# Delta-rule attention with a GELU layer: key norms read from the diagonal of the Gram blocks instead of from squares of K

## The chip, the cores and the metric

The kernel runs on one core of a Trainium2 chip. The metric is the device time of one execution in microseconds (us). The core has a matrix engine (PE, with its weight loads listed as PEld), a vector engine (DVE), a scalar engine (ACT), a general engine (POOL) and an engine that mostly issues transfers (SP). Each engine works through its own queue in order, and semaphores make one wait for another.

## The reference

```python
def _attn_ref(q, k, v, beta):                      # B=4, H=8, S=768, D=48
    k_n = k / (np.linalg.norm(k, axis=-1, keepdims=True) + 1e-06)
    state = np.zeros((B, H, D, D))
    for t in range(S):
        y[:, :, t] = einsum('bhd,bhde->bhe', q[:, :, t], state)
        v_old = einsum('bhde,bhd->bhe', state, k_n[:, :, t])
        state = state + beta_t * outer(k_n[:, :, t], v[:, :, t] - v_old)
# x = y as (3072, 384);  h = x @ w_in (384 x 2048);  out = gelu_exact(h) @ w_out (2048 x 384)
```

Every key is divided by its norm. The recurrence over 768 positions is solved in chunks, and its result goes through two matrix layers with an exact GELU between them. The two weights arrive as 64-bit numbers and are decoded to 32 bits on the chip.

## The kernel before

**Tiling.** The 768 positions are 12 chunks of 64. A chunk has two tiles, and a tile holds two batches: 2 x 64 positions on the 128 partitions, by eight heads. Two chunks in a row form a group, so a group has four tiles or 32 (tile, head) columns, and there are six groups, 0 to 5.

**One chunk.** `grams` multiplies the turned keys with themselves on PE (psG) and lets ACT copy the result: the off-diagonal 32 x 32 blocks into `G`, the diagonal ones into `diag` (L378, L382, L385). For a group, `eliminate_steps` inverts the triangular blocks on DVE. `flip` (L436) turns `diag` into `Nu`, so that one partition holds one whole 32 x 32 block as [row, column]. It is multiplied by `XM` (L437), which is the strict lower mask `low` times the row factors beta/norm^2, made on POOL (L431). Thirty row steps `eliminate(j)` follow, two DVE instructions each (L444, L446), then the diagonal is set to one, `weigh` multiplies by the column factors (L454), and `back` turns the result into `XM` and `Zf` (L460, L463). `top` copies part of `Zf` (L474), and `join` and `join_run` combine the 32-blocks to 64-blocks on PE (psJ).

**State.** `state_steps(w)` reads the state (psK, L578), forms `W` on DVE (L585), solves (psU), and computes outputs and the new state (psY; DVE adds `St`, L632, and `x`, L641). `turn` transposes `x` on PE (psX, L662) for the matrix layers.

**Norms before.** For groups 1 to 5 the norms come from squares of K: for chunks 2 and 3 ACT squares and sums head by head (L291, 32 times); for later chunks the keys are loaded a second time in natural layout (`Kn`), ACT squares a tile (L278), DVE sums it (L281), POOL takes the root as a power with exponent 0.5 (L306, 16 columns), and `factors` (L265 to L269) forms beta/norm^2. This is `prep` and `finish`, and it is done ahead of the Gram products. A small DVE transpose (L430) brings the factors into the layout of `Nu`. V is scaled by the norms on POOL or ACT (L332, L329). beta reaches its layout `beta_m` through 12 PE transposes in `signs`.

**Matrix layers.** For chunk c, `fc1` (psH, L684) and GELU on ACT (L686) make `G`. From chunk 2 on the second layer uses a scheme of seven products (psX, psZ, psY; L722) with additions on DVE: `mix` (L731 to L736) before the products, `read2` (L765 to L779) after. The last product into `psY` comes behind L768, which reads `psY` after the product before it.

**Order.** The start is written out by hand. The rest is a plan: each piece of work has a due time in units of chunks, and `emit` sorts by it. DVE keeps that order exactly; the other engines' orders come from a scheduler. I call step w the stretch with due times from w to w+1, in which the matrix layers of chunk w-1 run. In the trace step 3 is about 179 to 229 us, step 5 281 to 330, step 7 382 to 431, and step 9 483 to 532. In each of these four odd steps the elimination of a group (2, 3, 4, 5) runs on DVE between the other DVE work of the step; group 1 is eliminated at 120 to 149 us, behind the decoding of the weights, and group 0 at the start.

Of the kernel before, what the change touches and what calls it, by code (L numbers as in the profile page):

```python
# [8 lines left out]
F32 = mybir.dt.float32  # L9
U32 = mybir.dt.uint32  # L10
AX = mybir.AxisListType
ALU = mybir.AluOpType
# [4 lines left out]
def kernel(  # L17
# [28 lines left out]
    nc = tc.nc  # L46
    B, H, S, D = q.shape
    DM, DF = moe_w_in.shape
    C = 64
# [49 lines left out]
    for c in range(NC):  # L99
        for a in range(NA):  # L100
            u = tiles[c, a] = Unit()
            u.c, u.a, u.n = c, a, c * NA + a
            u.t = (c % 2) * NA + a
            if c < 4:
                u.Kp = u.Kn = Kp[u.n % NKS]
                u.Qp = Qp[u.n % NQS]
            else:
                u.Kn, u.Kp = Kp[2 + a], Kp[(4 if c % 2 == 0 else 0) + a]
                u.Kb, u.Qb = blocks_of[a], blocks_of[2 + a]
# [59 lines left out]
    nc.gpsimd.affine_select(out=low, in_=low, compare_op=ALU.is_ge, fill=0.0, base=-1,  # L169
# [4 lines left out]
    half = cpool.tile([128, NA * H], F32)  # L174
# [8 lines left out]
    beta_m = cpool.tile([128, NC, NA, H], F32)  # L183
# [71 lines left out]
    Ds, Gs, Nus, XMs, gms, ns = {}, {}, {}, {}, {}, {}  # L255
# [4 lines left out]
    def new_group(g):  # L260
        gms[g] = wk.tile([128, 2 * NA, H], F32, tag="gm", name="gm")

    def factors(gm, bt_, n):

        nc.vector.tensor_scalar_add(n, n, 1e-6)  # L265
        r = wk.tile([128, 2 * NA, H], F32, tag="r", name="r", bufs=1)[:, 0:n.shape[1]]
        nc.vector.reciprocal(r, n)
        nc.vector.tensor_tensor(gm, bt_, r, op=ALU.mult)
        nc.vector.tensor_tensor(gm, gm, r, op=ALU.mult)  # L269

    def squares(u, n, engine=None):
        kd = u.Kn[:, :, 0:D]
        if engine is nc.gpsimd:
            ksq = su.tile([128, H, D], F32, tag="w_e", name="ksq")
        else:
            ksq = wk.tile([128, H, D], F32, tag="ksq", name="ksq")
        if engine is None:
            nc.scalar.activation(ksq, kd, ACT.Square)  # L278
        else:
            engine.tensor_tensor(ksq, kd, kd, op=ALU.mult)  # L280
        nc.vector.tensor_reduce(n, ksq, axis=AX.X, op=ALU.add)  # L281

    def sum_of_squares(u, h):

        if "both" not in ns:
            n23 = wk.tile([128, 2 * NA, H], F32, tag="n0", name="n0", bufs=1)
            ns[2], ns[3] = n23[:, 0:NA], n23[:, NA:]
            ns["both"] = n23
        if h == 0:
            u.ksq = wk.tile([128, H, D], F32, tag="ksq", name="ksq")  # L290
        nc.scalar.activation(u.ksq[:, h], u.Kn[:, h, 0:D], ACT.Square,  # L291
                             accum_out=ns[u.c][:, u.a, h:h + 1])

    def prep(c):
        us = [tiles[c, a] for a in range(NA)]
        g = c // 2
        if c % 2 == 0:
            new_group(g)
        if c > 3:
            ns[c] = wk.tile([128, NA, H], F32, tag="n", name="n", bufs=4)  # L300
        n = ns[c]
        for u in us:
            if c > 3:
                squares(u, n[:, u.a])
        flat = n.rearrange("q a h -> q (a h)")
        nc.gpsimd.tensor_tensor(flat, flat, half, op=ALU.pow)  # L306

    def finish_both():
        factors(gms[1], beta_m[:, 2:4].rearrange("q c a h -> q (c a) h"), ns["both"])

    def finish(c):
        t = (c % 2) * NA
        factors(gms[c // 2][:, t:t + NA], beta_m[:, c], ns[c])
# [108 lines left out]
    def eliminate_steps(g):  # L422
        steps = []
        gts = []

        def scales():
            gt = wk.tile([128, HB], F32, tag="gt", name="gt", bufs=1)
            gts.append(gt)
            gl = XMs[g] = wk.tile([128, NU, HB], F32, tag="XM", name="XM", bufs=1)
            nc.vector.transpose(gt, gms[g].rearrange("q t h -> q (t h)"))  # L430
            nc.gpsimd.tensor_tensor(gl, low, gt.unsqueeze(2).to_broadcast([128, HB, HB]),  # L431
                                    op=ALU.mult)

        def flip():
            Nus[g] = wk.tile([128, HB, HB], F32, tag="Nu", name="Nu", bufs=1)
            nc.vector.transpose(Nus[g], Ds[g].rearrange("q u n -> q n u"))  # L436
            nc.vector.tensor_tensor(Nus[g], Nus[g], XMs[g], op=ALU.mult)  # L437
# [14 lines left out]
        def weigh():  # L452

            nc.vector.tensor_tensor(Nus[g], Nus[g],  # L454
                                    gts[0].unsqueeze(1).to_broadcast([128, HB, HB]), op=ALU.mult)
# [9 lines left out]
        steps = [(0.3, scales), (3.0, flip)]  # L465
# [5 lines left out]
    def top(g, p, us):  # L471

        part = Zf[g % 2][p * C:p * C + HB, us]
        nc.scalar.copy(part[:, :, 0:HB], part[:, :, HB:C])  # L474
# [365 lines left out]
    new_group(0)  # L840
# [12 lines left out]
    scales_, flip_, *rows, back0, back1 = [s_[1:] for s_ in eliminate_steps(0)]  # L853
    factors(gms[0], beta_m[:, 0:2].rearrange("q c a h -> q (c a) h"), n0)
    scales_[0]()
    flip_[0]()
    ng = wk.tile([128, NA, H], F32, tag="ng", name="ng", bufs=1)
# [3 lines left out]
    signs(2, NC)  # L861
# [32 lines left out]
    for p in range(2):  # L894
        top(0, p, EARLIER)
    for a in range(NA):
        join(0, (a,), 1)
    for p in range(2):
        top(0, p, LATER)
    for u in first[NA:]:  # L900
        scale_v(u)
    begin(0)
# [27 lines left out]
    def late():  # L930
# [3 lines left out]
        for a in range(NA):  # L934
# [3 lines left out]
            for c in range(5, NC, 2):  # L938
# [7 lines left out]
    sums = [(1.0, sum_of_squares, tiles[c, a], h) for c in (2, 3) for a in range(NA) for h in range(H)]  # L946
    plan += [at(1.08, 1.5, sums), at(1.51, 1.511, [(1.0, prep, c) for c in (2, 3)]), at(1.65, 1.655, [(1.0, finish_both)]), at(2.97, 2.971, [(1.0, finish, 4)]), at(2.725, 2.726, [(1.0, queries, third)]),
             at(1.12, 1.6, state_steps(1)),
             at(1.75, 2.45, eliminate_steps(1)),
             at(2.47, 2.6, top_steps(1, EARLIER) + top_steps(1, LATER)),  # L950
             at(2.64, 2.77, join_steps(1)), at(2.76, 2.985, state_steps(2)),
             at(2.72, 2.721, [(1.0, prep, 4)]), at(2.8, 2.9, [(1.0, grams, [tiles[4, a] for a in range(NA)])])]
# [5 lines left out]
    for c in range(4, NC):  # L958
# [5 lines left out]
        t = c - (2.1 if c % 2 == 0 else 2.6) if c > 5 else {4: 2.1, 5: 2.74}[c]  # L964
        plan += [at(t, t + 0.01, [(1.0, load_k, c, "Kn")])]
# [5 lines left out]
    for w in range(3, NC):  # L971
# [6 lines left out]
        if w % 2:  # L978
            plan += [at(w + 0.09, w + 0.092, gram + query), at(w + 0.25, w + 0.95, state_steps(w))]
            if two_ahead:  # L980
                rows = eliminate_steps(w // 2 + 1)
                plan += [at(w - 0.16, w - 0.15, [(1.0, prep, w + 2)]),
                         at(w, w + 0.01, [(1.0, finish, w + 2)]),
                         at(w + 0.13, w + 0.18, rows[:2]), at(w + 0.18, w + 0.36, rows[2:14]),
                         at(w + 0.4, w + 1.06, rows[14:-2]), at(w + 1.07, w + 1.16, rows[-2:]),
                         at(w + 1.17, w + 1.29, top_steps(w // 2 + 1, EARLIER)),
                         at(w + 1.305, w + 1.355, top_steps(w // 2 + 1, LATER))]
        else:
# [5 lines left out]
            if two_ahead:  # L994
                plan += [at(w + 0.35, w + 0.36, [(1.0, prep, w + 2)]),
                         at(w + 0.5, w + 0.51, [(1.0, finish, w + 2)])]
# [32 lines left out]
```

## Time and profile before

| | |
|---|---|
| median of three runs | 675.3 us (675.04 to 675.48) |
| the profiled execution, its own time | 674.69 us |
| its span, first to last instruction | 672.9 us |
| granted PE clock, mean | 0.982 |
| PE busy | 643.0 us (96%) |
| DVE busy | 419.9 us (62%) |
| ACT busy | 256.4 us (38%) |
| POOL busy | 75.8 us (11%) |

The page gives busy time by engine, the same in 40 slices of 16.8 us, the chain of work that ended last, and groups of instructions by line. A timeline row reads: start, duration, engine, line, operation, output <- input, count, and in brackets how long the engine stood idle ahead of it and what released it.

### The profile page before, as it was taken

Reading aid. Unit: us, or ns where it says so; the run is one execution under the profiler, and the core shown is the slowest. Engines: PE = TensorE matmul, PEld = TensorE weight load, DVE = VectorE, ACT = ScalarE, POOL = GpSimd, SP = SyncE. Lnnn points to the kernel's source line nnn. Section 1 sums busy time; section 2 is a strip of 40 time slices with the busy share of each in tenths; the row PEclk is TensorE's granted clock in tenths of the full one; section 3 lists DMA queues with packets and bytes.
Section 4 is the critical chain, followed back from the end, with each engine's and each line's share of the span. In section 5 each row is a group of like instructions: output and inputs, shape, how many; then the busy total and the mean of one; then the engine's idle time right before and its main releaser. Section 6 shows DMA issues by size and latency. Waiting matters only on the chain.

```text
span 672.9 us, 21675 instructions
## 1 busy us (share of the span) xinstructions
PE 643.0 (96%) x9542; PEld 562.7 (84%) x9542; DVE 419.9 (62%) x873; ACT 256.4 (38%) x654; POOL 75.8 (11%) x63
## 2 busy tenths in 40 slices
PE   6868999998999999999999999999999999999997
PEld 5656767766789989989989989989989979989997
DVE  6998989982699825479825479825479814324021
ACT  3477755624442173142173142173142153122220
POOL 4050301111211011111011111011111000000000
PEclk9976999998999999999999999999999999999999
DMA  8885655303531233511233411212301210100101
GB/s 119 186 251 172 120 165 136 48 1 56 91 50 31 50 47 54 84 27 31 51 47 56 82 26 31 48 21 35 63 3 31 50 18 3 24 2 2 23 1 24
DMA packets 158430, 39.75 MB, mean 59 GB/s; under 512 B 150016, under 2 KB 153216, under 8 KB 158336
## 3 DMA queue, kind: packets, MB, share of 16 engines
q1 hardware_dynamic: 152464, 33.40, 26.3%
q10 hardware_dynamic: 5872, 4.97, 3.2%
q8 instruction: 75, 1.23, 0.8%
q14 instruction: 19, 0.16, 0.1%
HBM read 33.62 MB, written 4.72 MB: 57 GB/s over the span
## 4 chain that ended last, share of the span: by engine, by line
PE 77%; DVE 14%; ACT 5%; issue 2%; DMA 1%; POOL 1%; SPq 0%; DVEq 0%; ACTq 0%; POOLq 0%
PE psH L684 32%; PE psX L722 12%; PE psY L722 12%; PE psZ L722 4%; PE psK L578 3%; DVE Nu L446 3%; DVE tmp L444 3%; PE psJ L525 3%; PE psG L367 3%; PE psU L600 2%; PE psO L697 2%; PE psY L618 2%; DVE w_e L235 1%; PE psY L627 1%; DVE w_out_sb L236 1%
## 5 line engine op out<-in xcount | busy, mean ns | idle before, releaser
L684 PE MATMUL psH<-xT,w_in_sb 128*128 128x256 f32 x1152 | 262.5, 384 | 3.8 <-ACT G L686 3.6
L684 PEld LDWEIGHTS psH<-xT,w_in_sb 128*128 128x128 f32 x1152 | 215.9, 190 | 35.9 <-ACT G L686 5.6
L686 ACT ACTIVATE G<-psH 128x256 f32<-128x256 f32 x192 | 73.2, 383 | 158.5 <-PE psH L684 157.6
L446 DVE TENSOR_TENSOR Nu<-Nu,tmp 128x30 f32<-128x30 f32 (+9 forms) x180 | 62.9, 349 | 6.2
L444 DVE TENSOR_TENSOR tmp<-Nu 128x30 f32<-128x30 f32 (+9 forms) x180 | 60.0, 333 | 5.2
L402 DVE TENSOR_TENSOR P<-psG,mask 128x1024 f32<-128x1024 f32 x10 | 12.2, 1224 | 80.4 <-PE psG L367 80.4
L722 PE MATMUL psX<-w_out_sb,G 128*128 128x192 f32 x320 | 56.2, 329 | 0.0
L722 PE MATMUL psY<-w_out_sb,G 128*128 128x192 f32 x304 | 54.1, 329 | 0.6
L722 PEld LDWEIGHTS psX<-w_out_sb,G 128*128 128x128 f32 x320 | 52.2, 190 | 0.7
L306 POOL TENSOR_TENSOR n<-n,half 128x16 f32<-128x16 f32 x10 | 29.4, 2944 | 197.9 <-DVE n L281 174.1
L663 ACT COPY xT<-psX 128x384 f32<-128x384 f32 x24 | 11.5, 479 | 105.2 <-PE psX L662 105.1
L722 PEld LDWEIGHTS psY<-w_out_sb,G 128*128 128x128 f32 x304 | 49.1, 190 | 2.1 <-DVE u L768 1.8
L697 PE MATMUL psO<-w_out_sb,G 128*128 128x384 f32 x128 | 45.7, 504 | 0.9 <-DVE w_out_sb L236 0.9
L697 PEld LDWEIGHTS psO<-w_out_sb,G 128*128 128x128 f32 x128 | 24.2, 196 | 16.0 <-DVE w_out_sb L236 1.5
L606 ACT COPY U<-psU 64x192 f32<-64x192 f32 x96 | 30.1, 314 | 19.5 <-PE psU L600 18.2
L332 POOL TENSOR_TENSOR V<-V,n 128x384 f32<-128x384 f32 x18 | 18.5, 1032 | 131.6 <-DMA V<-in_v_dram 92.7
L731 DVE TENSOR_TENSOR S<-G 128x512 f32<-128x512 f32 x20 | 14.4, 721 | 28.4 <-ACT G L686 28.4
L585 DVE TENSOR_TENSOR W<-psK,V 128x384 f32<-128x384 f32 x22 | 11.9, 554 | 31.3 <-ACT y L584 31.3
L641 DVE TENSOR_TENSOR x<-psY,y 64x192 f32<-64x192 f32 x80 | 28.3, 354 | 0.9
L722 PE MATMUL psY<-T,G 128*128 128x192 f32 x160 | 28.2, 329 | 0.0
L722 PE MATMUL psX<-T,G 128*128 128x192 f32 x160 | 28.1, 329 | 0.0
L722 PE MATMUL psZ<-T,S 128*128 128x192 f32 x160 | 27.6, 326 | 0.0
(138 smaller groups left out, 840.4 us busy)
## 6 DMA issues: line engine op xcount, KB each, us to landing
Kp<-in_k_dram SPq DMA_DIRECT2D x76, 96.0 KB, 3.3
w_out_sb<-in_moe_w_in_dram SPq DMA_DIRECT2D x24, 256.0 KB, 4.0
V<-in_v_dram SPq DMA_DIRECT2D x48, 96.0 KB, 3.1
out_dram<-o_sb ACTq DMA_DIRECT2D x46, 96.0 KB, 2.2
w_raw<-in_moe_w_out_dram SPq DMA_DIRECT2D x10, 384.0 KB, 4.6
Zf<-in_moe_w_out_dram SPq DMA_DIRECT2D x6, 384.0 KB, 4.2
Qp<-in_q_dram SPq DMA_DIRECT2D x64, 32.0 KB, 2.2
Qp<-in_q_dram SPq DMA_DIRECT2D x16, 96.0 KB, 3.8
```

Of the source, the lines that this page charges most:

```text
L306: nc.gpsimd.tensor_tensor(flat, flat, half, op=ALU.pow)
L367: nc.tensor.matmul(psG[HALF[p], r, i * NP + j, :], lhsT=u.Kt[rows, p, j, :], rhs=(u.Qt if x else u.Kt)[rows, p, j, :], start=True, stop=True)
L444: nc.vector.tensor_tensor(tmp, nu[:, j + 1:, j:j + 1].to_broadcast([128, n, j]), nu[:, j:j + 1, 0:j].to_broadcast([128, n, j]), op=ALU.mult)
L446: nc.vector.tensor_tensor(nu[:, j + 1:, 0:j], nu[:, j + 1:, 0:j], tmp, op=ALU.add)
L525: nc.tensor.matmul(psJ[to, i, :], lhsT=(xm if level else off)[rows, u, :], rhs=zf[rows, u, HB:C] if level else xm[rows, u, :], start=True, ...
L578: nc.tensor.matmul(u.psK[to, x, r, j, :], lhsT=(u.Qt if x else u.Kt)[rows, p, j, :], rhs=St[rows, u.a, p, j, :], start=True, stop=True)
L606: copy(pairs(u.U[HALF[p]], s), u.psU[HALF[p ^ s], p])
L641: nc.vector.tensor_tensor(dst, src, pairs(u.y[HALF[p ^ s]], s), op=ALU.add)
L684: nc.tensor.matmul(psH, lhsT=w_in_sb[:, f // 2, m, f % 2 * 128:(f % 2 + 1) * 128], rhs=xTs[c][:, m, :], start=(m == 0), stop=(m == NM - 1))
L686: nc.scalar.activation(G[:, f, :], psH, ACT.Gelu)
L697: nc.tensor.matmul(u.psO, lhsT=G[:, f, u.a * 128:(u.a + 1) * 128], rhs=w_out_sb[:, f, :], start=(f == 0), stop=(f == NF - 1))
L722: nc.tensor.matmul(ps_, lhsT=lhs[:, f, :], rhs=rhs[:, f, :], start=first and f == 0, stop=f == FH - 1, skip_group_check=not first)
```

## The change

In all groups but the first the norm of a key is read from the diagonal of its Gram block. `flip` now runs first, `norms` raises the 32 diagonal elements per partition of `Nu` to the power 0.5 on POOL, `scales` computes the factors in the turned layout, turns the norms back for V, and makes `XM`, and `scaled` multiplies the rows by the factors. The strict lower mask, now with its diagonal kept and combined with the column factors, is applied in `weigh`, behind the row steps. The second loads of K, the squares, their sums, `prep` and `finish` go away. beta of the later groups is loaded straight into the turned layout by 16 small transfers on SP's queue, issued after the keys of chunk 2 and ahead of the queries of chunk 2; ten PE transposes go. In the start, the `top` copies of group 0 move from ACT to DVE (first half) and POOL (second half). In the odd steps the due times become: flip and norms 0.11 to 0.12, scales 0.25, the mask-free scaling and four row steps 0.29 to 0.36, the other row steps and weigh 0.4 to 1.06; before, twelve row steps stood ahead of 0.36.

```diff
+    beta_t = cpool.tile([128, NG, HB], F32)
...
+    def load_beta():
+        for p in range(2):
+            for b in range(2):
+                for c in range(2):
+                    at_ = p * C + b * HB + c * NA * H
+                    for a in range(NA):
+                        src = beta[2 * a + p].rearrange("h (g t) -> h g t", t=2 * C)
+                        nc.sync.dma_start(out=beta_t[at_ + a * H:at_ + (a + 1) * H, 1:],
+                                          in_=src[:, 1:, c * C + b * HB:c * C + (b + 1) * HB])
...
         def flip():
             Nus[g] = wk.tile([128, HB, HB], F32, tag="Nu", name="Nu", bufs=1)
             nc.vector.transpose(Nus[g], Ds[g].rearrange("q u n -> q n u"))
-            nc.vector.tensor_tensor(Nus[g], Nus[g], XMs[g], op=ALU.mult)
+        def norms():
+            gts[g] = wk.tile([128, 2, HB], F32, tag="gt", name="gt", bufs=1)
+            flat = Nus[g].rearrange("q i c -> q (i c)")
+            nc.gpsimd.tensor_tensor(gts[g][:, 1], flat[:, 0:HB * HB:HB + 1], half, op=ALU.pow)
+        def scales():
...
+                factors(gts[g][:, 0], beta_t[:, g], gts[g][:, 1])
+                nc.vector.transpose(nat, gts[g][:, 1])
+            nc.gpsimd.tensor_tensor(gl, low, gts[g][:, 0].unsqueeze(1).to_broadcast([128, HB, HB]),
+                                    op=ALU.mult)
+        def scaled():
+            nc.vector.tensor_tensor(Nus[g], Nus[g],
+                                    gts[g][:, 0].unsqueeze(2).to_broadcast([128, HB, HB]), op=ALU.mult)
...
-            nc.vector.tensor_tensor(Nus[g], Nus[g],
-                                    gts[0].unsqueeze(1).to_broadcast([128, HB, HB]), op=ALU.mult)
+            nc.vector.tensor_tensor(Nus[g], Nus[g], XMs[g], op=ALU.mult)
...
-        steps = [(0.3, scales), (3.0, flip)]
+        steps = [(2.0, flip), (0.0, norms), (1.2, scales), (1.3, scaled)]
...
-    signs(2, NC)
+    load_beta()
...
     for p in range(2):
-        top(0, p, EARLIER)
+        top(0, p, EARLIER, nc.vector.tensor_copy)
...
+        top(0, p, LATER, nc.gpsimd.tensor_copy)
...
-    sums = [(1.0, sum_of_squares, tiles[c, a], h) for c in (2, 3) for a in range(NA) for h in range(H)]
-    plan += [at(1.08, 1.5, sums), at(1.51, 1.511, [(1.0, prep, c) for c in (2, 3)]), at(1.65, 1.655, [(1.0, finish_both)]),
+    second = eliminate_steps(1)
+    plan += [at(1.2, 1.21, second[:2]), at(1.5, 1.51, second[2:3]),
...
-        plan += [at(t, t + 0.01, [(1.0, load_k, c, "Kn")])]
...
-                plan += [at(w - 0.16, w - 0.15, [(1.0, prep, w + 2)]),
-                         at(w, w + 0.01, [(1.0, finish, w + 2)]),
-                         at(w + 0.13, w + 0.18, rows[:2]), at(w + 0.18, w + 0.36, rows[2:14]),
-                         at(w + 0.4, w + 1.06, rows[14:-2]), at(w + 1.07, w + 1.16, rows[-2:]),
+                plan += [at(w + 0.11, w + 0.12, rows[:2]), at(w + 0.25, w + 0.26, rows[2:3]),
+                         at(w + 0.29, w + 0.36, rows[3:8]),
+                         at(w + 0.4, w + 1.06, rows[8:-2]), at(w + 1.07, w + 1.16, rows[-2:]),
```

## The prediction

> **What bounds the kernel now.** I read the page's slices first, then busy time by stretch, then the timelines of DVE and PE inside one odd step, and last the queues of POOL and SP.
>
> The slices, PE and DVE:
>
> ```profile
> PE   6868999998999999999999999999999999999997
> DVE  6998989982699825479825479825479814324021
> ```
>
> The reader is to see that PE has spare time in the first slices only, and that DVE is nearly full in the 9s and 8s that come back every six slices. Those are the odd steps. Busy time by stretch (stretch, length, then PE, PEld, DVE, ACT, POOL, clock, DMA share, GB/s):
>
> ```profile
> 150.00:160.00 10.00, 6.72 (x180) 4.79 (x181) 0.59 (x1) 5.98 (x11) 2.34 (x1) 0.83 0.23 42
> 287.00:328.00 41.00, 40.88 (x570) 37.57 (x563) 35.33 (x84) 12.35 (x31) 3.89 (x3) 1.00 0.16 30
> 328.00:388.00 60.00, 60.00 (x1026) 54.14 (x1028) 27.96 (x58) 23.30 (x53) 7.99 (x4) 1.00 0.40 63
> ```
>
> From 160 us on PE is the bound and loses almost nothing (40.88 of 41, 60 of 60). So work taken from ACT, DVE or DMA there gains nothing, while whatever makes PE wait costs in full. PE waits 3.28 us at 150 us, behind the decoding and the elimination of group 1 on DVE. DVE in step 5:
>
> ```profile
> 289.43 1.99 DVE L436 STREAM_TRANSPOSE Nu<-diag 128x1024 f32<-128x1024 f32 x1
> 291.53 1.23 DVE L437 TENSOR_TENSOR Nu<-Nu,XM 128x1024 f32<-128x1024 f32 x1
> 292.79 0.21 DVE L444 TENSOR_TENSOR tmp<-Nu 128x30 f32<-128x30 f32 x1
> ...
> 302.44 0.69 DVE L731 TENSOR_TENSOR S<-G 128x512 f32<-128x512 f32 x1 [0.39 <-ACT G L686]
> ...
> 316.27 0.69 DVE L736 TENSOR_TENSOR G<-G 128x512 f32<-128x512 f32 x1 [0.61 <-PE psX L722]
> ...
> 326.61 0.36 DVE L768 TENSOR_TENSOR u<-psY,p 128x192 f32<-128x192 f32 x1 [1.44 <-PE psY L722]
> ```
>
> PE's next product starts at 327.03, right behind L768:
>
> ```profile
> 327.03 2.87 PE L722 MATMUL psY<-w_out_sb,G 128*128 128x192 f32 x16
> ```
>
> and the list of waits has it:
>
> ```profile
> PEld psY L722 <- DVE u L768: 1.8, 5, 0.4
> ```
>
> Between flip and L768 DVE stands idle for 0.39 + 0.61 + 1.44 = 2.44 us. That is all the delay an odd step can take before PE pays.
>
> **The odd steps.** In the changed order on DVE, `factors` stands directly behind `flip` and waits for POOL's power; nothing is between them, and the scaling, four row steps, W (L585) and the first additions for PE (L731) queue behind it. Flip cannot move up: it waits for the diag copy on ACT (L385, 288.16 + 1.24 = 289.40). Before, the root was taken a step ahead. The power's row, and POOL holding up DVE:
>
> ```profile
> L306 POOL TENSOR_TENSOR n<-n,half 128x16 f32<-128x16 f32 x10 | 29.4, 2944 | 197.9 <-DVE n L281 174.1 <-ACT ksq L291 23.9
> ```
>
> ```profile
> 305.58 1.04 POOL L332 TENSOR_TENSOR V<-V,n 128x384 f32<-128x384 f32 x1 [14.17 <-DVE Nu L446]
> ...
> 305.96 0.92 DVE L446 TENSOR_TENSOR Nu<-Nu,tmp 128x240 f32<-128x240 f32 x1
> ```
>
> - The power now has 32 columns. If its time were all fixed it would stay 2.9 us; if all per column it is 5.9. A POOL memset of 128x16 takes 0.11 us and a multiplication of 128x384 only 0.83, so little of the 2.9 is a fixed part, and I take 0.2 + 2 x 2.7 = 5.6 us.
> - The multiplication on POOL (XM, 1.92 us) is released together with the transpose of the norms and runs into the scaling. The row above shows a DVE instruction of 0.41 us stretched to 0.92 by the 0.66 us that POOL had left. With 1.7 us left I take 1.5 us; bounds 0 (before, XM ran beside flip and cost it nothing) and 1.9.
> - From flip's end to the first row step: signals 0.1 + 0.1, power 5.6, factors 0.97 (four instructions on 128x32 at 116.80 to 117.77), transpose 0.22, scaling 1.26, held up 1.5: 9.75 us, against 292.79 - 291.42 = 1.37 now. So 8.4 us later.
> - Ahead of L768 stand 25 row steps in place of 27. The two (130 and 108 wide) are 0.66 + 0.61 = 1.27 us.
> - PE pays 8.4 - 1.27 - 2.44 = **4.7 us** in step 5. Steps 7 and 9 have the same rows (DVE busy 35.35 and 35.31 of 41): 4.7 each.
> - In step 3 the gap before is 1.51 us, flip starts 0.15 earlier because `finish` is gone, and DVE idles only 0.94 us ahead of L768 (225.61): 9.75 - 1.51 - 0.15 - 1.27 - 0.94 = **5.9 us**.
> - In step 9 two instead of three copies of `top` (0.62 each) stand ahead of the GELU that PE waits for at 541.2 (1.54 us idle): -0.6.
>
> Sum 5.9 + 3 x 4.7 - 0.6 = **+19.4 us**. With the power at 2.9 it is 2.7 less in each step: +8.6. With that and no hold-up it is 1.7 + 3 x 0.5 - 0.6 = +2.6; with 5.9 and 1.9, +22.2.
>
> The Trainium skill (GPSIMD Engine Reference, section 3.1) puts two-input elementwise work at about 2.6 cycles per element. Read for the power, sixteen more columns would be an estimated 0.03 us, the power 2.9 us, and the whole 683 us by that rule against 694 by the row. But 16 columns in 2.9 us is far from that rate already, so I follow the row.
>
> **What goes away.** 16 squares on ACT (8.1 us), their sums on DVE (16 x 0.54), eight `finish` of 0.9 us, 32 key loads of 96 KB. From 160 us on these lie in stretches where PE is full and DVE and ACT are not (27.96 and 23.30 of 60), so I cost their loss at nothing; the loads land in 3.3 us and no engine's wait names them. The V scaling (L332) follows XM on POOL, which now ends near 300 us, before V at 305.58.
>
> **The start.** Until 153 us the chain is DVE's.
>
> - ACT loses 32 small squares that follow each other at 0.225 us (7.3 us). DVE waits for ACT's part of the decoding 0.50, 0.91 and 1.57 us; the last (87.82) vanishes, since `flip` of group 1 now sits in the decoding and fills it, and so does the 0.26 us wait for XM at 120.10: -1.8. All of DVE's idle from 45 to 121 us but a 1.15 us transfer wait would be some -4; that is the bound.
> - XM of group 1 now meets decoding: +1.5 (0 to 1.9).
> - Two squares between `top` and the join copies (151.14, 0.94 us): -0.9. Ten PE transposes at 18.8 us: nothing, PE idles there.
> - 16 beta transfers on SP. Rows of SP (start, time for all, count):
>
> ```profile
> 23.51 5.04 SPq L96 DMA_DIRECT2D Qp<-in_q_dram  x4
> 28.65 2.64 SPq L96 DMA_DIRECT2D Qp<-in_k_dram  x4
> 72.67 8.65 SPq L134 DMA_DIRECT2D Qp<-in_k_dram  x16
> 96.40 0.81 SPq L210 DMA_DIRECT2D w_raw<-in_moe_w_out_dram  x2
> ```
>
> An issue costs 0.40 to 0.54 us, so the queries of chunk 2, the keys of chunk 3, the weights and V behind them move back by 6.4 to 8.6 us. The keys land about 3.3 us after their issue, and PE turns them at 38.12 to 40.09 us: 0 to 3 us late, 1.6 in the middle. Behind them the Gram copies on ACT, and then XM's join copies (44.24), shift by as much; two `top` copies off ACT give 0.85 back ahead of the solve. +0.8 (-0.9 to +2.2). The later weights are decoded from 56 us on, still after they land.
> - Two `top` copies on DVE (on ACT 0.62 each): 1.2 to 2 us, covered by the 0.50 and 0.91 us waits; uncovered, up to +2.
>
> Sum -1.8 + 1.5 - 0.9 + 0.8 = -0.4, say -0.5, from -4.9 to +4.
>
> **Total.** +18.9 us on the profiled execution (674.69 us, 1.8 of it outside its span). The median lies 0.6 above it: 675.3 + 18.9 = **694**.
>
> **Rivals.**
> 1. *The power does not grow with the columns.* For it: ten powers at 2.90 us, almost to the ns, as a fixed part would give. Against: nothing else on POOL has a fixed part over 0.2 us. 675.3 + 8.6 - 0.5 = 683.
> 2. *Faster: the start gains more than the odd steps lose.* ACT's relief in the first 150 us removes DVE's waits, -4.9. It decides only where the odd steps cost less than that, so with a power below about 3.5 us and no hold-up by XM: 675.3 + 2.6 - 4.9 = 673. For it: 13.4 us of ACT work leaves a stretch in which PE and DVE wait for ACT. Against: the 2.44 us of slack.
> 3. *SP's queue decides the start.* Beta's issues wait for earlier landings too and push the keys of chunk 3 by 4 us and more: start +4 in place of -0.5: 698.5.
> 4. *The norms path is hidden after all*, if DVE had other work behind `flip`. The order on DVE has none, so I give it no chance of its own.
>
> **How the numbers follow.** Forecast 0.58, rival 1 0.17, rival 2 0.13 (0.09 of it faster, 0.04 within), rival 3 0.12. A measurement of this kernel tells about 0.2% (1.4 us) from no change. Faster 0.09, same 0.04, slower 0.87. The range goes from between rivals 2 and 1, 678, to just above rival 3, 700, and leaves out rival 2 and the tails. The forecast's own range is 690 to 699.
>
> **What would show it.** Right: the power row at 5 to 6 us on 128x32; DVE idle that long behind each `flip`, released by POOL; PE waiting for the addition to `u` in steps 3, 5, 7 and 9, with its busy share falling from 40.88 of 41 to about 41 of 46; the even steps unchanged. Wrong: a power near 3 us, or PE full in the odd steps. For the start: PE's wait at 150 us near 3 us as before, and a later first join if SP decides. The forecast fails most simply if the power has a large fixed part.

## The result: 3.5% slower, and the profile after

The changed kernel takes 698.57 us in the median (698.33 to 700.30, four runs), the kernel before beside it 675.39 us (675.04 to 675.55). The ratio is 1.0349, with a 95% interval from 1.0331 to 1.0367. The forecast was 694, with a range from 678 to 700.

The profiled execution of the changed kernel has a span of 696.6 us, 23.7 more than before. Where they lie is read by lining the two traces up at the state products (psK), which open the state part of every step. Difference of their starts, changed minus before:

| between | adds (us) |
|---|---|
| start of the trace and step 2 (psK at 163.18 before) | -1.73 |
| step 3 | +7.13 |
| step 5 | +5.76 |
| step 7 | +6.70 |
| step 9 | +5.81 |
| steps 4, 6, 8, 10 and the end, together | +0.05 |

So all of the loss is in the four odd steps, as forecast, and it is 25.4 us where the forecast had 19.4. Slices of PE and DVE of the changed kernel:

```profile
PE   6768999999997999999899999799999799999998
DVE  7999999943779815369924369825349934414121
```

PE now dips to 7 or 8 in one slice at each place where DVE has its 9s and 8s; before, it stood at 9 there. Busy time by stretch of the changed kernel, an even step and an odd one (columns as in the prediction):

```profile
236.00:288.00 52.00, 52.00 (x922) 47.04 (x921) 22.98 (x38) 20.26 (x46) 0.00 (x0) 1.00 0.35 53
288.00:343.00 55.00, 51.38 (x662) 46.47 (x662) 41.17 (x97) 13.75 (x35) 11.98 (x6) 0.97 0.14 27
```

The even step is full, the odd step has lost 3.6 us of PE and some of its clock (0.97). The power's row among the groups:

```profile
L409 POOL TENSOR_TENSOR gt<-Nu,half 128x32 f32<-128x32 f32 x5 | 27.4, 5475 | 358.3 <-DVE Nu L403 358.3
```

and the rows that are new in the list of waits (engine, tile and line, releaser, then the sum, the count and the longest):

```profile
DVE gt L274 <- POOL gt L409: 22.5, 4, 5.6
...
PE psY L711 <- DVE u L754: 7.2, 4, 1.8
PE psX L651 <- DVE x L630: 6.9, 4, 1.8
```

The power takes 5.5 us where 16 columns took 2.94, DVE stands still for it 5.6 us in each odd step, and PE waits twice for DVE at each odd step's end, for `x` (L641 before) and for the first of two additions to `u` (L765 before). Timeline of DVE behind `flip` in step 5 (L403 is flip, L274 begins the factors, L426 is the scaling, L434 and L436 are the row steps, L574 is W):

```profile
294.86 1.97 DVE L403 STREAM_TRANSPOSE Nu<-diag 128x1024 f32<-128x1024 f32 x1 [0.22 <-ACT diag L362]
302.45 0.18 DVE L274 TENSOR_SCALAR gt<-gt 128x32 f32<-128x32 f32 x1 [5.62 <-POOL gt L409]
...
303.52 1.21 DVE L426 TENSOR_TENSOR Nu<-Nu,gt 128x1024 f32<-128x1024 f32 x1
304.76 2.23 DVE L434 TENSOR_TENSOR tmp<-Nu 128x30 f32<-128x30 f32 x1
307.03 0.77 DVE L436 TENSOR_TENSOR Nu<-Nu,tmp 128x30 f32<-128x30 f32 x1
307.83 0.76 DVE L434 TENSOR_TENSOR tmp<-Nu 128x58 f32<-128x58 f32 x1
...
309.94 1.01 DVE L574 TENSOR_TENSOR W<-psK,V 128x384 f32<-128x384 f32 x2
```

and the timeline of POOL in the same stretch:

```profile
296.98 5.44 POOL L409 TENSOR_TENSOR gt<-Nu,half 128x32 f32<-128x32 f32 x1 [87.02 <-DVE Nu L403]
303.64 3.31 POOL L422 TENSOR_TENSOR XM<-low,gt 128x1024 f32<-128x1024 f32 x1 [1.22 <-DVE n L421]
306.91 1.61 POOL L309 TENSOR_TENSOR V<-V,n 128x384 f32<-128x384 f32 x2
```

The first three row instructions take 2.23, 0.77 and 0.76 us; alone they take 0.21, 0.21 and 0.22. They are over when POOL's three multiplications are. Timeline of PE at the end of step 5, where it now waits twice:

```profile
330.91 0.55 PE L651 MATMUL psX<-ident,x 128*128 128x128 f32 x3 [1.70 <-DVE x L630]
333.26 4.51 PE L711 MATMUL psY<-w_out_sb,G 128*128 128x192 f32 x16 [1.80 <-DVE u L754]
...
338.21 2.87 PE L711 MATMUL psY<-w_out_sb,G 128*128 128x192 f32 x16
```

Sixteen of the same products take 4.51 us behind the two waits, and the next sixteen take 2.87 us.

### The profile page after: what moved, and what is told of

The parts are those of the page before. It is cut to its first block, busy times and chain, and to the rows that moved or that the text cites. A ratio compares the mean times of both kernels' runs of the same rounds, so it can differ in the third digit from the quotient of the medians.

```text
span 696.6 us, 21515 instructions
## 1 busy us (share of the span) xinstructions
PE 654.0 (94%) x9532; PEld 570.1 (82%) x9532; DVE 423.4 (61%) x843; ACT 239.6 (34%) x568; POOL 79.9 (11%) x60
## 4 chain that ended last, share of the span: by engine, by line
PE 55%; DVE 33%; ACT 4%; issue 3%; POOL 3%; DMA 1%; SPq 0%; POOLq 0%; ACTq 0%; DVEq 0%
PE psH L673 21%; PE psY L711 11%; DVE tmp L434 9%; DVE Nu L436 7%; PE psX L711 7%; POOL gt L409 3%; PE psJ L514 3%; PE psG L344 2%; PE psZ L711 2%; PE psK L567 2%; PE psO L686 2%; DVE Nu L403 2%; DVE x L630 2%; DVE w_e L236 1%; DVE w_out_sb L237 1%
## 5 line engine op out<-in xcount | busy, mean ns | idle before, releaser
L434 DVE TENSOR_TENSOR tmp<-Nu 128x30 f32<-128x30 f32 (+9 forms) x180 | 73.2, 407 | 5.2
L711 PE MATMUL psY<-w_out_sb,G 128*128 128x192 f32 x304 | 62.1, 362 | 7.7 <-DVE u L754 7.2
L409 POOL TENSOR_TENSOR gt<-Nu,half 128x32 f32<-128x32 f32 x5 | 27.4, 5475 | 358.3 <-DVE Nu L403 358.3
L436 DVE TENSOR_TENSOR Nu<-Nu,tmp 128x30 f32<-128x30 f32 (+9 forms) x180 | 62.5, 347 | 6.2
L711 PEld LDWEIGHTS psY<-w_out_sb,G 128*128 128x128 f32 x304 | 56.3, 212 | 10.1 <-DVE u L754 8.2
L574 DVE TENSOR_TENSOR W<-psK,V 128x384 f32<-128x384 f32 x22 | 11.8, 554 | 31.3 <-ACT y L573 31.3
L711 PEld LDWEIGHTS psZ<-T,S 128*128 128x128 f32 x160 | 26.2, 190 | 1.8 <-DVE S L720 1.7
```

Of the source, the lines that this page charges most:

```text
L409: nc.gpsimd.tensor_tensor(gts[g][:, 1], flat[:, 0:HB * HB:HB + 1], half, op=ALU.pow)
L434: nc.vector.tensor_tensor(tmp, nu[:, j + 1:, j:j + 1].to_broadcast([128, n, j]), nu[:, j:j + 1, 0:j].to_broadcast([128, n, j]), op=ALU.mult)
L436: nc.vector.tensor_tensor(nu[:, j + 1:, 0:j], nu[:, j + 1:, 0:j], tmp, op=ALU.add)
L711: nc.tensor.matmul(ps_, lhsT=lhs[:, f, :], rhs=rhs[:, f, :], start=first and f == 0, stop=f == FH - 1, skip_group_check=not first)
```

## The experiments

All kernels below start from the changed kernel, and the short diffs are against it; "g < 2" and "g > 1" in them leave the start and group 1 as they are. Times are medians, ratios are against the kernel before on the same chip; the last column is what steps 3, 5, 7 and 9 add to the time before, read as in the table above. Five of the expectations below were missed by much: the root left out, the root for V only, both edits together and the early Gram products, which by their traces share one oversight (DVE idle ahead of W), and V on ACT.

| kernel | us | ratio (95%) | steps 3, 5, 7, 9 |
|---|---|---|---|
| changed kernel | 698.57 | 1.0349 (1.0331 to 1.0367) | 7.13, 5.76, 6.70, 5.81 |
| root left out | 684.00 | 1.0141 (1.0123 to 1.0160) | 2.63, 2.60, 2.68, 2.70 |
| root twice (two runs) | 718.77 | 1.0653 (1.0631 to 1.0674) | 12.32, 11.31, 11.18, 11.24 |
| column factors on DVE | 686.26 | 1.0175 (1.0153 to 1.0197) | 4.89, 3.39, 3.44, 2.37 |
| root for V only | 688.67 | 1.0208 (1.0193 to 1.0224) | 3.99, 3.85, 3.83, 3.89 |
| both of these | 687.79 | 1.0189 (1.0167 to 1.0212) | 3.83, 3.85, 3.84, 3.06 |
| Gram products early | 694.16 | 1.0290 (1.0254 to 1.0326) | 7.94, then see below |
| twelve rows ahead of W, alone | 704.70 | 1.0430 (1.0413 to 1.0447) | 8.67, 7.41, 7.20, 7.27 |
| twelve rows, root for V only | 682.71 | 1.0104 (1.0089 to 1.0119) | 3.15, 1.81, 1.81, 1.77 |
| twelve rows, both edits | 672.64 | 0.9961 (0.9948 to 0.9974) | 0.87, 0.01, 0.00, -1.38 |
| the same, V scaled on ACT | 681.82 | 1.0090 (1.0074 to 1.0105) | 2.22, 2.11, 2.14, 0.85 |

### The price of the root: left out, and taken twice

```diff
-            nc.gpsimd.tensor_tensor(gts[g][:, 1], flat[:, 0:HB * HB:HB + 1], half, op=ALU.pow)
+            nc.gpsimd.tensor_tensor(gts[g][:, 1], flat[:, 0:HB * HB:HB + 1], half, op=ALU.mult)
```

> The root of the squared norms is left out (POOL multiplies the 32 columns by 0.5 in place of raising them to the power 0.5), so the factors and V are scaled wrongly; everything else is the changed kernel. Theory (the wait behind flip makes the time, and the power is what is waited for): flip's end to the first row step falls by about 5.3 us in every odd step, the product that waits for u comes earlier by nearly as much, and the whole lands at 675 to 679 us in place of 698.6; PE's granted clock stays at 1.00 in the odd steps, because PE no longer stands still. Rival (POOL's multiplications that hold up DVE make the time, the power lies mostly in DVE's spare time): the whole stays above 688 us.

Measured 684.00 us. POOL's instruction now takes 0.26 us and DVE waits 0.44 us for it. The odd steps fall by 3 to 4.5 us each, less than the 5.3 taken away, and 2.6 us of each stay. PE's clock is back at 1.00 in step 5, though PE still waits there, 0.84 and 1.61 us for the two additions to `u`. The wait is thus the largest part and not the whole. What stays is POOL's hold-up of the row steps, as long as before (2.23, 0.77 and 0.76 us), and 1.9 us of idle time on DVE ahead of W and of the first addition for PE. The second kernel does the power two times:

```diff
-            nc.gpsimd.tensor_tensor(gts[g][:, 1], flat[:, 0:HB * HB:HB + 1], half, op=ALU.pow)
+            for _ in range(2):
+                nc.gpsimd.tensor_tensor(gts[g][:, 1], flat[:, 0:HB * HB:HB + 1], half, op=ALU.pow)
```

> The power is taken twice in a row on POOL in groups 1 to 5 (the second of the same input, so the result is the same). Theory: each odd step is longer by the full 5.4 us, since its spare time is used up already; 698.6 + 4 x 5.4 = 720.4 us. If a longer standstill of PE costs it more clock behind the standstill, some 1 to 2 us more in each step, up to 728. Rival (the power is partly hidden): below 715.

Measured 718.77 us: 20.2 us more for 4 x 5.5 us of added waiting. Nearly nothing of the wait is hidden. PE's granted clock does fall further (mean 0.940 in the profiled execution, 0.966 in that of the changed kernel), but no time comes on top for it. Another wait shows up, of the solve (psU) for W, in the timeline of PE in step 5:

```profile
321.12 1.96 PE L590 MATMUL psU<-W,Zf 64*64 64x48 f32 x64 [3.46 <-DVE W L575]
323.01 4.71 PE L712 MATMUL psX<-w_out_sb,G 128*128 128x192 f32 x16
```

Again the products behind the wait are slow: 4.71 us instead of 2.87.

### POOL's multiplication taken away

```diff
         def scales():
...
-            nc.gpsimd.tensor_tensor(gl, low, gts[g][:, 0].unsqueeze(1).to_broadcast([128, HB, HB]),
-                                    op=ALU.mult)
+            if g < 2:
+                nc.gpsimd.tensor_tensor(gl, low, gts[g][:, 0].unsqueeze(1).to_broadcast([128, HB, HB]),
+                                        op=ALU.mult)
...
         def weigh():
-            nc.vector.tensor_tensor(Nus[g], Nus[g], XMs[g], op=ALU.mult)
+            if g < 2:
+                nc.vector.tensor_tensor(Nus[g], Nus[g], XMs[g], op=ALU.mult)
+            else:
+                nc.vector.tensor_tensor(Nus[g], Nus[g], low, op=ALU.mult)
+                nc.vector.tensor_tensor(Nus[g], Nus[g],
+                                        gts[g][:, 0].unsqueeze(1).to_broadcast([128, HB, HB]), op=ALU.mult)
```

> In groups 2 to 5 the multiplication of the mask by the column factors on POOL is taken away; weigh does two multiplications on DVE instead of one, 1.2 us more, behind the last addition that PE waits for. Theory (POOL's multiplication holds up DVE's first row steps): the first three instructions of the row steps fall from 2.23, 0.77 and 0.76 us to about 0.2 each, unless the scaling of V, which then starts 3 us earlier, takes the place; each odd step is 2 to 3 us shorter, the whole 686 to 691. Rival (the hold-up is all of it): about 677. Rival (DVE's stretched instructions cost PE nothing): 698 to 699.

Measured 686.26 us, at the lower end of what was expected. DVE's first row instructions in step 5 take 0.70, 0.77 and 0.22 us; the scaling of V, which now stands right behind the power, holds the first two. Each odd step is 2.2 to 3.4 us shorter. In step 9, 1.2 of the 3.4 us have another source: PE waits 0.39 us in place of 1.59 for a GELU near the step's end, because ACT now does five GELUs and not four ahead of the `top` copies. The rest stays, so the hold-up is a cause in its own right.

### The wait taken away

The factor is beta / norm^2, and the squared norm is on the diagonal. No root is needed for it.

```diff
         def norms():
...
+            r = wk.tile([128, HB], F32, tag="r", name="r", bufs=1)
+            nc.vector.tensor_copy(gts[g][:, 1], flat[:, 0:HB * HB:HB + 1])
+            nc.vector.reciprocal(r, gts[g][:, 1])
+            nc.vector.scalar_tensor_tensor(gts[g][:, 0], beta_t[:, g], -1.0, r, ALU.mult, ALU.mult)
+            nc.gpsimd.tensor_tensor(gts[g][:, 1], gts[g][:, 1], half, op=ALU.pow)
...
         def eliminate(j):
             nu = Nus[g]
+            if g > 1 and j == 8:
+                nc.vector.tensor_scalar_add(gts[g][:, 1], gts[g][:, 1], 1e-6)
+                nc.vector.transpose(gts[g, "nat"], gts[g][:, 1])
```

The norms are turned back in front of the eighth row step (j == 8), not the ninth as the expectation has it.

> In groups 2 to 5 the factors come from the reciprocal of the squared norm itself (the 1e-6 added to the norm is dropped there), three short instructions on DVE right behind flip; POOL's power follows and serves only the scaling of V, and its result is turned in front of the ninth row step. Theory: the wait of 5.6 us behind flip is gone, flip's end to the first row step is 2 to 2.5 us, the hold-up by POOL stays; the whole 676 to 681 us. Rival (POOL's power, now beside DVE's row steps, holds these up for its 5.4 us): 690 or more.

And this edit and the one before it together:

> The two edits together in groups 2 to 5: the factors from the reciprocal of the squared norm (no wait for the power; the 1e-6 added to the norm is dropped there), and the mask and column factors by two multiplications on DVE in weigh (no multiplication on POOL). Theory: nothing is left that delays DVE by more than the 2.4 us that it has spare, PE does not wait in the odd steps, and only the 1.7 us that the start gained remain: 673 to 674.5 us, faster than the kernel before by 0.1 to 0.3%. If the scaling of V on POOL still holds DVE up by more than that: 675 to 680.

Measured 688.67 and 687.79 us: both far above the expectation, worse than leaving out the root, and next to nothing is gained by taking POOL's multiplication away as well. Timeline of DVE in step 5 of the second of the two (L447 and L449 are the row steps, L592 is W):

```profile
296.14 0.20 DVE L447 TENSOR_TENSOR tmp<-Nu 128x30 f32<-128x30 f32 x1
...
298.00 0.27 DVE L449 TENSOR_TENSOR Nu<-Nu,tmp 128x108 f32<-128x108 f32 x1
302.81 0.56 DVE L592 TENSOR_TENSOR W<-psK,V 128x384 f32<-128x384 f32 x1 [4.54 <-ACT y L591]
```

The row steps begin 2.13 us behind flip's end, unstretched, and then DVE stands still again, 4.54 us in front of W. In the changed order only four row steps stand ahead of W; before it was twelve. W cannot start before ACT has copied what PE makes at 301 us. The 5.6 us of waiting for POOL have turned into 4.5 us of waiting for ACT, and the eight row steps that could fill them stand behind it. POOL's multiplication fell into that idle time (299.94 to 302.30 in the kernel with the root for V only), and so it cost nothing there.

### Gram products earlier

```diff
-            plan += [at(w + 0.09, w + 0.092, gram + query), at(w + 0.25, w + 0.95, state_steps(w))]
+            ahead = gram if w > 3 else []
+            plan += [at(w - 0.09, w - 0.088, ahead)]
+            plan += [at(w + 0.09, w + 0.092, (gram if w == 3 else []) + query), at(w + 0.25, w + 0.95, state_steps(w))]
...
-                plan += [at(w + 0.11, w + 0.12, rows[:2]), at(w + 0.25, w + 0.26, rows[2:3]),
+                t = -0.06 if w > 3 else 0.11
+                plan += [at(w + t, w + t + 0.01, rows[:2]), at(w + 0.25, w + 0.26, rows[2:3]),
```

> The changed kernel with the Gram products of steps 5, 7 and 9 due 0.18 of a step earlier, ahead of the last product of the step before, and flip and the power with them; step 3 stays as it is. Theory (nothing is wrong with the power itself, only nothing stands on DVE while it runs): flip ends about 6 us earlier, in time in which DVE stands idle anyway, the power is over when DVE comes to the factors, and steps 5, 7 and 9 fall from +5.8, +6.7 and +5.8 us to 0 to 1.5 each, while step 3 stays at +7.1; the whole 680 to 685 us. Rival (a wait for the earlier Gram products takes its place on PE or DVE): above 690.

Measured 694.16 us: a miss. DVE does not wait for the power any more in steps 5, 7 and 9, and these cost 2.56, 2.55 and 2.80 us. But in front of each of them 3.86, 1.96 and 1.98 us are lost. (The profiled execution took 698.09 us and was the slowest of the four; in front of its step 5 PE waits 2.00 us, and the granted clock is 0.89 from 285 to 300 us.) Ahead of its step 7 the timeline of PE has

```profile
397.04 0.55 PE L651 MATMUL psX<-ident,x 128*128 128x128 f32 x3 [0.88 <-ACT xT L652]
```

and in that step the timeline of DVE has

```profile
417.00 0.56 DVE L574 TENSOR_TENSOR W<-psK,V 128x384 f32<-128x384 f32 x1 [3.46 <-ACT y L573]
```

ACT's Gram copies now stand between the copies (xT) that PE's last products of the step before wait for, and DVE idles in front of W as above, because there are four row steps to do.

### The order ahead of W

```diff
-                         at(w + 0.29, w + 0.36, rows[3:8]),
-                         at(w + 0.4, w + 1.06, rows[8:-2]), at(w + 1.07, w + 1.16, rows[-2:]),
+                         at(w + 0.29, w + 0.36, rows[3:16]),
+                         at(w + 0.4, w + 1.06, rows[16:-2]), at(w + 1.07, w + 1.16, rows[-2:]),
```

This diff stands in all four kernels of this part. First alone, with the wait and POOL's multiplication as they are:

> The changed kernel with its wait, and twelve row steps ahead of W in place of four, nothing else. Theory (the four go with the wait: behind 5.6 us of waiting there is no time for more ahead of W): W comes some 5 us later than now, PE waits in front of the solve as well, and two more row steps stand ahead of the last addition to u; each odd step is 1.2 to 3 us longer, the whole 703 to 711 us. Rival (the order alone is the cost): 690 or less.

Measured 704.70 us, as expected by the theory. PE waits for W in front of the solve, 17.9 us in all four steps together, 4.16 in step 5. So four row steps are the better number as long as the wait is there: the order and the wait belong together. Then without the wait, POOL's multiplication still there ("the run with that multiplication on DVE" is the one after this):

> Factors from the reciprocal of the squared norm in groups 2 to 5 (the 1e-6 dropped there), twelve row steps ahead of W, and the multiplication by the column factors still on POOL, behind the power. Theory: against the run with that multiplication on DVE, POOL's 3.3 us now meet the row steps ahead of W and hold them up by 2 to 3 us, more than is spare: each odd step costs 2 to 3 us, the whole 681 to 686. Rival (the hold-up falls into spare time): 673 to 676.

Measured 682.71 us. POOL and DVE meet in front of W in step 5. Timeline of POOL:

```profile
294.76 5.43 POOL L416 TENSOR_TENSOR gt<-gt,half 128x32 f32<-128x32 f32 x1 [83.17 <-DVE r L414]
300.15 2.43 POOL L431 TENSOR_TENSOR XM<-low,gt 128x1024 f32<-128x1024 f32 x1
```

and of DVE (L441 adds the 1e-6 for V's norms):

```profile
296.13 0.20 DVE L446 TENSOR_TENSOR tmp<-Nu 128x30 f32<-128x30 f32 x1
...
300.28 2.34 DVE L441 TENSOR_SCALAR gt<-gt 128x32 f32<-128x32 f32 x1
```

Beside the power DVE's row steps run at their usual 0.20 us. Beside the multiplication an instruction of 0.17 us takes 2.34, to the end of POOL's. Now without either:

> As the run without the wait and without POOL's multiplication (factors from the reciprocal of the squared norm in groups 2 to 5, the 1e-6 dropped there; mask and column factors on DVE in weigh), and now twelve row steps stand ahead of W, as in the kernel before, in place of four. In that run DVE stood idle 4.54 us ahead of W, because only four row steps stood there. Theory (wait, hold-up and the order ahead of W together make the odd steps' cost): the idle time ahead of W fills with eight row steps of about 0.6 to 0.8 us; DVE is then later than in the kernel before by 0.7 us at the first row step, 0.4 for turning the norms and about 1.2 for four scalings of V on POOL in place of two, 2.3 us against 2.4 us that are spare. Each odd step costs 0 to 0.7 us, the whole is 673 to 676 us. Rival (something else in the new order costs, such as the instructions behind W): 680 or more.

Measured 672.64 us (671.52 to 673.86, seven runs), just below the expected range and 0.39% faster than the kernel before (0.26 to 0.52%). Step 5 is as full as before in busy time (columns as above):

```profile
285.00:327.00 42.00, 41.89 (x625) 38.19 (x623) 35.88 (x85) 12.13 (x32) 8.96 (x5) 1.00 0.11 22
```

and in its timeline DVE waits for PE again, and not PE for DVE:

```profile
326.60 0.36 DVE L775 TENSOR_TENSOR u<-psY,p 128x192 f32<-128x192 f32 x1 [0.86 <-PE psY L729]
```

DVE has 0.86 us to spare ahead of the addition that PE waits for; before it had 1.44 there. This is the version that beats both. Its lead of 2.9 us over the kernel before is not explained in full, and what the traces show of it is not the norms. The span of its profiled execution is only 1.1 us shorter than before: the start gives 0.91 us, within its own spread (see below), and step 9 gives 1.38, while steps 3, 5 and 7 add 0.88 and the even steps 0.31. In step 9 it is PE's wait for the GELU that falls, from 1.54 to 0.36 us. In all four kernels with both multiplications of `weigh` on DVE, ACT does five GELUs ahead of the `top` copies there, and this wait is 0.32 to 0.39 us; in all the others ACT does four, and it is 1.54 to 1.62. So that gain goes with an order on ACT that came along with the edit and was not its aim. Taking POOL's multiplication away was worth 0.9 us with four row steps ahead of W (less than those two runs can tell apart) and 10.1 us with twelve, some 1.2 of these by that order. The last step was to take V off POOL too ("the first of these four" is the run of 672.64 us):

```diff
-  plan += [at(c - 0.4, c - 0.3, v_steps(c)) for c in range(4, NC)]
+  plan += [at(c - 0.4, c - 0.1, [(1.0, scale_head, tiles[c, a], h)
+                                 for a in range(NA) for h in range(H)]) for c in range(4, NC)]
```

> As the first of these four, and V of chunks 4 to 11 is scaled on ACT, head by head, in place of POOL. Theory: the last hold-up of DVE by POOL in the odd steps goes (about 2.2 us), DVE has spare time again, PE waits nowhere in the odd steps, and the whole is 672.5 to 674.5 us, 0.1 to 0.4% faster than the kernel before. If the 64 small scalings hold up ACT's GELUs between PE's products: 675 to 680.

Measured 681.82 us, a little worse than the second of the two cases named. ACT waits 2.91 us for V to land (306.41) with GELUs queued behind it, and the timeline of PE shows the wait for ACT:

```profile
307.52 1.56 PE L691 MATMUL psH<-xT,w_in_sb 128*128 128x256 f32 x6 [1.40 <-ACT G L693]
```

### The start

Beta's transfers moved behind the weights and V:

```diff
-    load_beta()
     for u in first:
         transposed(u, (1,))
...
     load_v(1)
+    load_beta()
```

> The changed kernel with the 16 beta transfers issued behind the weights and V of the start in place of ahead of the queries of chunk 2. Theory (SP's queue delays loads that PE can wait for, and the start is set by DVE): PE's waits for the queries and keys of chunk 2 and 3 at 34 to 39 us go, the first state product moves by less than 0.5 us and the whole by less than 1 us: 697.8 to 698.7. Rival (the beta transfers cost the start): 696 to 697.

The four `top` copies of group 0 back on ACT:

```diff
-        top(0, p, EARLIER, nc.vector.tensor_copy)
+        top(0, p, EARLIER)
...
-        top(0, p, LATER, nc.gpsimd.tensor_copy)
+        top(0, p, LATER)
```

> The changed kernel with the four copies of top of group 0 back on ACT. Theory: they are worth the 0.5 us by which the first solve came earlier, and the wait of DVE for ACT that covers it afterwards; the whole is longer by 0 to 1 us: 698.6 to 699.6. Rival (DVE pays for its two copies): shorter by up to 1.5 us.

Measured 699.29 us (698.58 to 700.18) and 697.97 us (696.60 to 700.41), ratios 1.0363 (1.0345 to 1.0380) and 1.0343 (1.0318 to 1.0368). The first lies 0.6 us above its expected range, the second in that of its rival, and neither can be told from the changed kernel's 1.0349. With the transfers late PE's waits for the loads go, as expected, and the Gram products start at 38.34 us in place of 40.02; but the first join behind them starts at 43.14 in both, when DVE has `XM` ready. The start itself is not the same from one profile to the next: in the profiles of the changed kernel and of the eight others whose edits leave the start alone (without the two of the root, which change group 1), the psK of step 2 comes 0.24 to 3.40 us earlier than before. So for either edit the intervals rule out an effect of more than some 3 us on the whole, and what is smaller stays open.

## Why the prediction was right, point by point

The total was right (698.57 in the range of 678 to 700, and just inside the forecast's own 690 to 699), and so were the mechanism and its place. That the total came as near as this is partly luck, since errors cancel: in step 5 the forecast had DVE 1.8 us too late at the first row step and nothing for 3.3 us of hold-up behind it, and the start gained 1.2 us more than it had. By the total alone rival 3 (698.5) would have been right; the profile decides against it, for the loss lies in the odd steps.

| step 5, us | forecast | measured |
|---|---|---|
| power of 32 columns | 5.6 | 5.44 |
| flip's end to the first row step | 9.75 (1.5 of it hold-up) | 7.93 (294.86 + 1.97 to 304.76) |
| later than before by | 8.4 | 6.6 |
| further hold-up of DVE by POOL, more than before | 0 | 3.3 |
| two row steps fewer | -1.27 | -1.13 |
| spare time of DVE | -2.44 | -2.44 (none is left) |
| DVE late at the last addition to u (L757, L768 before) | 4.7 | 5.8 (40.97 behind flip's end, 35.19 before) |

The terms of the right column (6.6, 3.3, -1.13 and -2.44) add up to 6.3; neighbouring rows overlap by up to 0.1 us at their ends, so a sum of rows is off by some tenths.

- **The power grows with the columns.** Right: 2.94 us for 16, 5.44 for 32, that is 0.16 us a column and 0.4 fixed. Rival 1 falls. Its ten powers "at 2.90 us, almost to the ns" were nine; one, at 77.71 us, took 3.32. The figure of the Trainium skill (GPSIMD Engine Reference, section 3.1: about 2.6 cycles per element) would have left the power near 2.9 by the prediction's estimate; the measurement decides against it for this operation.
- **POOL holds up DVE.** The mechanism was right, but the term was too small and in the wrong place: 1.5 us for the scaling, with 1.9 as the upper bound. The scaling (1.21 us) was not held at all. It had started 0.12 us ahead of POOL's multiplication, which took 3.31 us where it had taken 1.91, as if it waited for the scaling's end; then DVE's first row instruction waited for POOL. Two scalings of V right behind cost another 1.1. The forecast had V follow only at 305.58, where it cost nothing more than before. Taking the multiplication alone away gave 12 us (686.26).
- **PE pays what DVE is late.** Right for step 5, though PE does not wait where the forecast had it, at the last addition to `u`, but ahead of it: twice, 1.70 and 1.80 us, and the next 16 products then take 4.51 us. In step 5 DVE comes to the last addition no earlier than these end, so this hides. In step 7 the products take 5.49 us, DVE waits 1.03 us for them, and the step costs 6.70. The forecast had no term for it. The difference of about 0.9 us between steps 5 and 7 is not fixed to a place: in the two kernels of the start step 9 is dear (6.66 and 6.67), and step 3 has 7.95 and 7.94 in place of 7.13. It goes with PE's clock. Over 20 us at the end of a step the mean granted clock is 0.83 in every dear step (step 7 here, steps 3 and 9 in those two) and 0.91 in all the others of the three kernels. With a clock of one half in between, that is about 6.8 and 3.6 us of slow clock (twice the missing share of 20 us).
- **Step 3 costs more than step 5**: forecast by 1.2, measured by 1.4. **Step 9 costs 0.6 less**: not seen, and the reading behind it was wrong. Two copies of `top` in place of three do stand ahead of that GELU, but they start when DVE has `Zf` ready, and PE still waits 1.59 us (1.54 before). In the best version three copies stand there, and the wait is 0.36, because ACT does one GELU more ahead of them (see above).
- **Even steps unchanged, no cost for what is gone**: right, +0.05 us together.
- **The start**: PE is busy for 8.45 of the 10 us behind 150, where it was 6.72; its wait for the join there is 1.55 us in place of 3.28. Forecast -0.5, measured -1.73 in the profile. Group 1's elimination ends 0.77 us earlier on DVE (147.80 against 148.57), and the two squares in front of the join copies were worth 0.96. The two waits of DVE forecast to vanish (at 87.82 and 120.10) did; POOL's multiplication held a decoding instruction for 2.0 us (2.99 instead of 0.96), forecast 1.5. Beta's transfers took 7.08 us on SP (forecast 6.4 to 8.6) and made PE wait for the queries and keys, 1.09, 1.50 and 0.47 us, but the Gram products of the keys start at 40.02 in both traces. So rival 3 falls, and rival 2 with its short power as well. How much of the 1.2 us between forecast and measurement is the start's own spread is open.
- **A rival's price was wrong.** The forecast priced a kernel with a short power and no hold-up at +2.6 us in the odd steps (rival 2). The kernel with no wait and no multiplication on POOL has even less for DVE to wait for, and its odd steps cost 14.6. The forecast counted the row steps ahead of L768 (25 for 27) and not those ahead of W (4 for 12). As long as DVE waits for POOL this does not matter. Without that wait it is nearly all that is left, and only with twelve row steps back ahead of W does the time fall below the kernel before.

## What to carry to other kernels

On an engine that works in order, a wait is paid until something else sets the same end: before pricing its removal, look for the next instruction that has a fixed earliest time (here W, which needs PE's product through ACT) and count the work that stands ahead of that one, not only ahead of the end. Price single edits in the order in which they would stay: one and the same edit was worth 1 us, 10 us or 12 us, depending on what else was there. And a value that is needed squared does not have to wait for its root: the root can follow for the consumer that has time.

## What the runs showed of the hardware that was not expected

**PE's clock behind short waits.** In the changed kernel PE waits 1.70 and 1.80 us with 0.55 us of work between. Stretches of it behind these waits, in steps 5 and 7 (columns as above, the granted clock is third from the end, in front of the DMA share):

```profile
333.00:338.00 5.00, 4.74 (x19) 4.58 (x19) 4.56 (x14) 0.00 (x0) 0.00 (x0) 0.66 0.00 0
...
440.00:445.30 5.30, 5.28 (x16) 5.19 (x17) 4.13 (x12) 0.00 (x0) 0.00 (x0) 0.50 0.02 3
```

PE is busy and runs at 0.66 and 0.50. In the kernel without wait and multiplication, four row steps ahead of W, PE waits 1.80 and 1.62 us in steps 3, 5 and 7, with 2.87 us of products between, and the clock behind the waits in step 5 is 1.00. But in step 9 of the same execution the first of these waits is enough. Timeline of PE, and the stretch around it:

```profile
538.53 4.55 PE L729 MATMUL psY<-w_out_sb,G 128*128 128x192 f32 x16 [1.80 <-DVE u L772]
```

```profile
536.00:546.00 10.00, 8.00 (x38) 7.40 (x38) 9.21 (x29) 1.25 (x3) 0.00 (x0) 0.83 0.05 11
```

So the length of the waits alone does not decide it in these runs. Where PE waits 4.16 us for W (twelve rows alone), the products behind take 4.79 us. The Trainium skill (TensorE: Matmul & The Clock Gate, Part 1) says that the clock falls to one half after an idle window of about 3.4 us and that the window's place is not fixed to the program. The half agrees (0.50), and so do the 3.6 and 6.8 us of slow clock worked out above, about one and two such windows. That a wait of 1.80 us can be enough does not agree with a whole idle window, and here the measurement decides; whether the place of the window makes the difference between steps no run here shows. What these runs add is the price. The 16 products behind such waits take 1.6 to 2.6 us more. Where DVE is late anyway, little of it is seen in the time: in the kernel with the root for V only, step 3 has it (4.55 us for the 16 products) and costs 3.99, and steps 5 and 7 do not and cost 3.85 and 3.83. Where it lasts twice as long, it costs 0.8 to 1.1 us more (steps 3, 7 and 9 of the changed kernel against the same steps of the two kernels of the start).

**POOL's power does not hold up DVE, POOL's multiplication does.** Both work on tiles in SBUF. Beside the power DVE's row steps keep their 0.20 us; beside the multiplication a DVE instruction waits until POOL has ended (2.23 us for 0.21, 2.34 for 0.17, 2.99 for 0.96). The Trainium skill (SBUF — State Buffer, Who interferes with whom) has an exclusive lock between the two engines, held for a whole instruction by whichever starts first, when DVE's instruction has two inputs in SBUF and POOL's reads SBUF. The 2.23 and the 2.99 agree with it; the 2.34 is of an instruction with one input (TENSOR_SCALAR), which this condition does not cover. The power reads SBUF too, and does not agree; no run here shows why.
